# The last two layers of an attention, soft-MoE and feed-forward kernel: the elementwise work of a tile goes over the scalar engine or the vector engine, and GpSimd has no part in it

## The chip, the cores and the metric

The kernel runs on one core of a Trainium2 chip. The metric is the time of one execution in microseconds (us), as the median of several runs. One execution is also taken by the hardware profiler; its rows are what is read below. The engines are TensorE (PE in the rows, PEld for its weight loads), VectorE (DVE), ScalarE (ACT), GpSimd (POOL) and SyncE (SP, which only issues transfers here).

## The reference

Three stages follow one another: causal attention with a memory term, a soft mixture of experts, and a feed-forward block of two layers with a squared relu. The change lies in the last one.

```python
def reference(...):
    x = attention(q, k, v, M_prev, z_prev, beta)      # 4 x 8 heads, 576 tokens, 64 wide
    x = x.transpose(0, 2, 1, 3).reshape(2304, 512)
    # soft mixture: 32 slots over 8 experts of 4
    logits = x @ phi                                  # 2304 x 32
    slot_out = experts(softmax(logits, axis=0).T @ x) # 32 x 512
    x = softmax(logits, axis=1) @ slot_out            # 2304 x 512
    # feed-forward block: w_in 512 x 2048, w_out 2048 x 512, s and b one number each
    h = x @ w_in
    r = np.maximum(h, 0.0)
    g = s * (r * r) + b
    return (g @ w_out).astype(np.float32)
```

`w_in` and `w_out` come as 64-bit floats.

## The kernel before

The kernel has three stages in order of time. The attention stage (0 to about 250 us) goes over 16 pairs of heads in an order that is written out by hand. The experts' weights are streamed through from about 215 to 302 us. The stage of the last two layers, to which the change belongs, fills the rest. In the first and the last of these GpSimd has elementwise work; it can't read the matmul's sums (PSUM) and works from SBUF only.

**The last two layers.** The product of the mixture with `w_in` is folded: `G` (32 slots by 2048, kept with a high and a low part) is `slot_out @ w_in`, made in six pieces by `g_piece`. A *tile* is 128 hidden units (one `k` of 16) for 384 tokens (one group `g` of 6), so there are 96 tiles. `seq` sets their order: first groups 0 and 1 interleaved (`k` = 0 for both, then `k` = 1, ...: 32 tiles), then groups 2 to 5 one after another (16 tiles each).

For a tile, `first` does one matmul (128x384, line L770) into a PSUM buffer `h`, of which there are two, and then the elementwise work: relu, square, times `s`, plus `b`. The result is needed as two rounded parts, `hi` and `lo` = result − `hi`, since the second matmuls run on rounded 32-bit data (fp32r). `second` then does nine matmuls of 512 columns (L799, L800, L801: three blocks of 128 tokens, each `hi` with the high part of `w_out`, `hi` with its low part, `lo` with the high part), which add up over the 16 `k` in PSUM. Behind the last `k` of a group three copies (L200) bring the sums to SBUF and three transfers write them out.

`P` in the rows is the work buffer `r` of a tile, and `R` the ring of `hi` and `lo`, both with NB = 4 places. `second` is called for the tile three behind that of `first` (AHEAD = 3).

Before the change a letter in the table `cp` says how the elementwise work of a tile is split, by `k` and by group (the third word holds for groups 2 to 5):

- "d": relu on ScalarE (L774), then three operations on VectorE (L785, L786, L787).
- "p": relu and square on ScalarE (L774, L776), then affine step, rounding copy and subtraction on GpSimd (L781, L261, L264).
- "q": the same with the rounding copy on ScalarE (L778), and two operations on GpSimd (L779, L264).

There are 58 tiles of the first kind, 31 of the second and 7 of the third.

**The decoding of `w_out`.** Between the first 32 tiles, `decode_out` turns `w_out` from 64-bit to 32-bit floats in eight rounds of two `k` each: one operation on ScalarE (L181), four on VectorE (L183, L185, L187, L189; 128x1024, the first round in halves), and then for each `k` a rounding copy on ScalarE (L758, the high part) and a subtraction on VectorE (L759, the low part). The buffers are `raw` and `PT` for the 64-bit words, `Q0` and `Q1` for the result, and `w` for both parts. The table `dc` says ahead of which tile a round is called, `gp` the same for the pieces of `G`.

**The order.** In this stage a scheduler sets the order of the instructions of each engine when the program is built, from the code's order and from when it expects operands to be ready; on the chip each engine takes its instructions in that fixed order and waits where an operand isn't there. Where a copy is left open (`evac` with no engine named), it also picks ScalarE or VectorE.

Of the kernel before, what the change touches and what calls it, by code (L numbers as in the profile page):

```python
# [12 lines left out]
AF = mybir.ActivationFunctionType  # L13
ALU = mybir.AluOpType
# [31 lines left out]
T = dict(  # L46
    warm=1,
    wt=[3, 4, 4, 4, 3, 3],
    cp=['pppddppppppqpqqq', 'dpdpppdpqdqddddq', 'pddpddddddddddpp'],
    NB=4,  # L50
    sim=0,
    ge='aaaaaa',
    gc='ananaa',
    dc=[-1, 3, -1, 10, 10, 16, 22, 20],
# [17 lines left out]
def strided(ap, *dims):  # L72

    return bass.AP(ap.tensor, ap.offset, [list(ap.ap[0])] + [list(d) for d in dims])
# [3 lines left out]
def tile_attention_moe_ffn(  # L78
# [16 lines left out]
    PE, ACT, DVE, POOL, SP = nc.tensor, nc.scalar, nc.vector, nc.gpsimd, nc.sync  # L95
# [9 lines left out]
    sbt = keep.tile([128, 2], F32, name="sbt")  # L105
# [149 lines left out]
    def load_rest(p):  # L255
        if p < NPAIR:
            qvm_t[p] = QA[p % 3]
            SP.dma_start(out=qvm_t[p], in_=qvm[p])

    def pool_copy(dst, src):  # L260
        POOL.tensor_scalar(out=dst, in0=src, scalar1=1.0, scalar2=0.0, op0=ALU.mult, op1=ALU.add)  # L261

    def pool_sub(dst, a, b):
        POOL.tensor_tensor(out=dst, in0=a, in1=b, op=ALU.subtract)  # L264

    def feature(p, part):
        q = qvm_t[p][:, 0:S]
# [355 lines left out]
    def ps_h():  # L623
        return pH.tile([128, 512], F32, tag="h", name="h")
# [62 lines left out]
    for b in range(B):  # L687
# [14 lines left out]
            out=csk[:, :, 1:4:2, :], in0=strided(cex[:, 0, 0:1], (NSLOT, 5), (0, 2), (1, NSLOT)),  # L702
            in1=strided(chi[:, 0, 0:1], (NSLOT, 5), (0, 2), (1, NSLOT)), op=ALU.subtract)
# [14 lines left out]
    def G(c0, n):  # L718
        return RC[c0 // 1024][:, c0 % 1024:c0 % 1024 + n]
# [48 lines left out]
    def first(n, g, k):  # L768
        hp = ps_h()
        PE.matmul(hp[:, 0:TG], G(k * 128, 128), cT[:, g * TG:(g + 1) * TG], start=True, stop=True)  # L770
        i = n % NB
        r = PC[:, TG * i:TG * (i + 1)]
        hi, lo = ring[2 * i:2 * i + 2]
        ACT.activation(out=r, in_=hp[:, 0:TG], func=AF.Relu)  # L774
        if T["cp"][min(g, 2)][k] in "pq":
            ACT.activation(out=r, in_=r, func=AF.Square)  # L776
            if T["cp"][min(g, 2)][k] == "q":
                ACT.activation(out=hi, in_=r, func=AF.Identity, scale=sbt[:, 0:1], bias=sbt[:, 1:2])  # L778
                POOL.tensor_scalar(out=r, in0=r, scalar1=sbt[:, 0:1], scalar2=sbt[:, 1:2], op0=ALU.mult, op1=ALU.add)  # L779
            else:  # L780
                POOL.tensor_scalar(out=r, in0=r, scalar1=sbt[:, 0:1], scalar2=sbt[:, 1:2], op0=ALU.mult, op1=ALU.add)  # L781
                pool_copy(hi, r)
            pool_sub(lo, r, hi)
        else:
            DVE.scalar_tensor_tensor(out=r, in0=r, scalar=sbt[:, 0:1], in1=r, op0=ALU.mult, op1=ALU.mult)  # L785
            DVE.tensor_scalar(out=hi, in0=r, scalar1=sbt[:, 1:2], scalar2=0.0, op0=ALU.add, op1=ALU.add)  # L786
            DVE.scalar_tensor_tensor(out=lo, in0=r, scalar=sbt[:, 1:2], in1=hi, op0=ALU.add, op1=ALU.subtract)  # L787
        g_t[g, k] = (hi, lo)
# [23 lines left out]
    for i in range(-1, len(seq) + AHEAD):  # L812
        for k2 in range(8):
            if T["dc"][k2] == i:
                decode_out(k2)
        for j in range(6):
            if T["gp"][j] == i:
                g_piece(j)
        if 0 <= i < len(seq):
            first(i, *seq[i])  # L820
        if i >= AHEAD:
            second(*seq[i - AHEAD])
# [63 lines left out]
```

## Time and profile before

| what | value |
|---|---|
| median of 3 runs | 555.32 us (553.84 to 561.74) |
| the profiled execution | 555.2 us, span of its instructions 553.4 us |
| mean granted clock of TensorE | 0.987 of full speed |
| TensorE busy | 520.3 us (94%) |
| VectorE busy | 365.5 us (66%) |
| ScalarE busy | 280.4 us (51%) |
| GpSimd busy | 172.3 us (31%) |

The span runs from the first to the last instruction; the execution's own time lies 1.8 us above it. A share of busy time is a mean over stages that have different limits, and matmuls are pipelined, so that their rows overlap. What counts for the change is the stretch from about 305 us on.

### The profile page before, as it was taken

To read this page: it belongs to the slowest core of one execution; us is meant where nothing else is said; L and a number is where in the kernel's file an instruction comes from. 1 tells how busy PE (TensorE), PEld (TensorE's weight loads), DVE (VectorE), ACT (ScalarE), POOL (GpSimd) and SP (SyncE) were. 2 spreads that over 40 slices of the span, in tenths; PEclk is the share of its full clock that TensorE was granted. 3 is DMA by queue.
4 is the path that set the end of the run, shared out by engine and by line. 5 is a ranking of instruction groups with operands and counts; after the bars stand their busy time and mean duration, and the time that the engine had idled before them with its cause. 6 is when DMAs were issued, how large, how long until landed. Compare 5 with 4: busy or idle time off the path is not lost.

```text
span 553.4 us, 9319 instructions
## 1 busy us (share of the span) xinstructions
PE 520.3 (94%) x3255; PEld 345.3 (62%) x3255; DVE 365.5 (66%) x917; ACT 280.4 (51%) x743; POOL 172.3 (31%) x212
## 2 busy tenths in 40 slices
PE   3999999999999999989999788879999999999997
PEld 1466665666566656653332456558888888888885
DVE  2788887888788878750430999983367465473770
ACT  2877777777777767510221765453542422423322
POOL 0233331332233333300000469996430411404103
PEclk9999999999999999997999999898999999999999
DMA  8799342424242413789995342400020010100101
GB/s 263 249 334 343 126 148 72 150 72 149 69 152 72 149 50 115 245 300 381 368 358 181 126 153 76 152 1 1 1 114 1 10 48 0 59 0 1 57 1 57
DMA packets 26622, 72.01 MB, mean 130 GB/s; under 512 B 3024, under 2 KB 3152, under 8 KB 26576
## 3 DMA queue, kind: packets, MB, share of 16 engines
q1 hardware_dynamic: 26576, 71.42, 37.2%
q8 instruction: 26, 0.43, 0.3%
q14 instruction: 20, 0.16, 0.1%
HBM read 66.69 MB, written 4.72 MB: 129 GB/s over the span
## 4 chain that ended last, share of the span: by engine, by line
PE 84%; POOL 7%; DVE 4%; issue 2%; DMA 1%; ACT 1%; SPq 0%; POOLq 0%; DVEq 0%; ACTq 0%
PE y L799 10%; PE y L801 10%; PE y L800 10%; PE s L290 9%; PE t L335 8%; PE o L394 7%; PE s L364 4%; PE y L662 3%; PE s L294 3%; PE y L646 3%; POOL P L781 3%; PE h L770 3%; POOL R L264 2%; PE t L338 2%; PE t L429 2%
## 5 line engine op out<-in xcount | busy, mean ns | idle before, releaser
L801 PE MATMUL y<-w,R 128*128 128x512 f32 x288 | 114.2, 397 | 6.0 <-POOL R L264 6.0
L799 PE MATMUL y<-w,R 128*128 128x512 f32 x288 | 115.7, 402 | 3.9 <-POOL R L261 3.6
L800 PE MATMUL y<-w,R 128*128 128x512 f32 x288 | 114.1, 396 | 1.4 <-DVE w L759 1.4
L774 ACT ACTIVATE P<-h 128x384 f32<-128x384 f32 x96 | 47.1, 492 | 123.9 <-PE h L770 123.9
L781 POOL TENSOR_SCALAR P<-P,sbt 128x384 f32<-128x384 f32 x31 | 34.7, 1120 | 194.6 <-ACT P L776 194.6
L785 DVE SCALAR_TENSOR_TENSOR P<-P,sbt 128x384 f32<-128x384 f32 x58 | 45.0, 776 | 58.6 <-ACT P L774 58.4
L316 ACT ACTIVATE P<-P,st 128x256 f32<-128x256 f32 (+3 forms) x128 | 71.0, 556 | 5.8 <-DVE st L302 5.8
L801 PEld LDWEIGHTS y<-w,R 128*128 128x128 f32 x288 | 54.6, 190 | 23.3 <-POOL R L264 9.8
L799 PEld LDWEIGHTS y<-w,R 128*128 128x128 f32 x288 | 54.7, 190 | 18.9 <-POOL R L261 6.7
L302 DVE CUSTOM_DVE_ANT_0 P<-s,cs 128x128 f32<-128x128 f32 (+3 forms) x128 | 58.7, 480 | 10.5 <-PE s L290 6.1
L800 PEld LDWEIGHTS y<-w,R 128*128 128x128 f32 x288 | 54.9, 191 | 10.9 <-DVE w L759 1.7
L335 PE MATMUL t<-cs,P 128*128 128x128 f32 x320 | 46.1, 282 | 0.8 <-DVE raw L204 0.6
L290 PE MATMUL s<-R,Q 64*128 64x256 f32 (+3 forms) x176 | 36.8, 499 | 9.5 <-DMA R<-in_qk_dram 8.8
L264 POOL TENSOR_TENSOR R<-P,R 128x384 fp32r<-128x384 f32 x38 | 43.2, 1138 | 3.2
L335 PEld LDWEIGHTS t<-cs,P 128*128 128x128 f32 x320 | 34.2, 141 | 14.4 <-DVE x L417 8.0
L787 DVE SCALAR_TENSOR_TENSOR R<-P,sbt,R 128x384 fp32r<-128x384 f32 x58 | 36.9, 636 | 5.8 <-DVE R L786 0.5
L329 POOL TENSOR_SCALAR P<-P,st 128x576 f32<-128x576 f32 x16 | 16.2, 1014 | 67.1 <-DVE st L325 51.5
L770 PE MATMUL h<-x,R 128*128 128x384 f32 x96 | 34.4, 358 | 0.6 <-ACT P L774 0.6
L202 ACT ACTIVATE raw<-t 128x128 f32<-128x128 f32 (+2 forms) x64 | 25.5, 432 | 15.4 <-PE t L335 15.4
L423 POOL TENSOR_TENSOR x<-x,M 128x512 f32<-128x512 f32 x15 | 19.2, 1280 | 44.4 <-DVE x L417 44.4
L202 ACT ACTIVATE PT<-t 128x128 f32<-128x128 f32 (+2 forms) x64 | 25.2, 433 | 10.4 <-PE t L335 10.4
L786 DVE TENSOR_SCALAR R<-P,sbt 128x384 fp32r<-128x384 f32 x58 | 26.4, 455 | 5.9
(232 smaller groups left out, 868.9 us busy)
## 6 DMA issues: line engine op xcount, KB each, us to landing
w<-in_w_dram SPq DMA_DIRECT2D x18, 512.0 KB, 7.1
raw<-in_w_in_dram SPq DMA_DIRECT2D x8, 1024.0 KB, 5.4
w<-in_w_dram SPq DMA_DIRECT2D x32, 256.0 KB, 5.4
Q<-in_qvm_dram SPq DMA_DIRECT2D x11, 673.0 KB, 5.6
R<-in_qk_dram SPq DMA_DIRECT2D x32, 144.0 KB, 2.8
out_dram<-P SPq DMA_DIRECT2D x18, 256.0 KB, 2.0
raw<-in_w_out_dram SPq DMA_DIRECT2D x4, 1024.0 KB, 4.8
R<-in_qvm_dram SPq DMA_DIRECT2D x5, 673.0 KB, 6.5
```

Source lines behind the costliest of these rows:

```text
L202: ACT.activation(out=dst, in_=src, func=AF.Copy)
L264: POOL.tensor_tensor(out=dst, in0=a, in1=b, op=ALU.subtract)
L290: PE.matmul(ps[:, 512 * h:512 * h + n], q[r, t * 128:(t + 1) * 128], k[r, 0:n], start=True, stop=True)
L302: DVE.tensor_tensor_reduce(out=Pt[h, t], in0=x, in1=cs[:, C_M2 - n:C_M2], scale=-0.125, scalar=BIG, op0=ALU.add, op1=ALU.min, accum_out=st ...
L316: ACT.activation(out=pt, in_=pt, func=AF.Exp, scale=-1.0, bias=st[:, 18 + c:19 + c], accum_out=st[:, c:c + 1])
L335: PE.transpose(tp[:, kb * 128:(kb + 1) * 128], Pt[i, t][:, kb * 128:(kb + 1) * 128], ident)
L770: PE.matmul(hp[:, 0:TG], G(k * 128, 128), cT[:, g * TG:(g + 1) * TG], start=True, stop=True)
L774: ACT.activation(out=r, in_=hp[:, 0:TG], func=AF.Relu)
L781: POOL.tensor_scalar(out=r, in0=r, scalar1=sbt[:, 0:1], scalar2=sbt[:, 1:2], op0=ALU.mult, op1=ALU.add)
L799: PE.matmul(acc[g, i], hi[:, c], who[k], start=(k == 0), stop=False)
L800: PE.matmul(acc[g, i], hi[:, c], wlo[k], start=False, stop=False)
L801: PE.matmul(acc[g, i], lo[:, c], who[k], start=False, stop=(k == NK - 1))
```

## The change

The table `cp` gets other words, and the kinds "p" and "q" are replaced by one kind "a": relu, square, affine step and rounding copy on ScalarE, and one subtraction on VectorE. The kind "d" stays as it is. In the first 32 tiles three of four `k` are "a" in both groups; in the groups 2 to 5 "a" and "d" alternate. That makes 56 "a" and 40 "d" tiles. The two GpSimd helpers go.

```diff
 T = dict(
...
-    cp=['pppddppppppqpqqq', 'dpdpppdpqdqddddq', 'pddpddddddddddpp'],
+    cp=['aaadaaadaaadaaad', 'aaadaaadaaadaaad', 'adadadadadadadad'],
...
-    def pool_copy(dst, src):
-        POOL.tensor_scalar(out=dst, in0=src, scalar1=1.0, scalar2=0.0, op0=ALU.mult, op1=ALU.add)
-
-    def pool_sub(dst, a, b):
-        POOL.tensor_tensor(out=dst, in0=a, in1=b, op=ALU.subtract)
...
         ACT.activation(out=r, in_=hp[:, 0:TG], func=AF.Relu)
-        if T["cp"][min(g, 2)][k] in "pq":
+        if T["cp"][min(g, 2)][k] == "a":
             ACT.activation(out=r, in_=r, func=AF.Square)
-            if T["cp"][min(g, 2)][k] == "q":
-                ACT.activation(out=hi, in_=r, func=AF.Identity, scale=sbt[:, 0:1], bias=sbt[:, 1:2])
-                POOL.tensor_scalar(out=r, in0=r, scalar1=sbt[:, 0:1], scalar2=sbt[:, 1:2], op0=ALU.mult, op1=ALU.add)
-            else:
-                POOL.tensor_scalar(out=r, in0=r, scalar1=sbt[:, 0:1], scalar2=sbt[:, 1:2], op0=ALU.mult, op1=ALU.add)
-                pool_copy(hi, r)
-            pool_sub(lo, r, hi)
+            ACT.activation(out=r, in_=r, func=AF.Identity, scale=sbt[:, 0:1], bias=sbt[:, 1:2])
+            ACT.activation(out=hi, in_=r, func=AF.Copy)
+            DVE.tensor_tensor(out=lo, in0=r, in1=hi, op=ALU.subtract)
         else:
```

The lines behind the removed helpers move up by 6, and those of the "d" kind and of `second` by 10. In the changed file an "a" tile has L768 (relu), L770 (square), L771 (affine step), L772 (rounding copy) and L773 (subtraction); a "d" tile L768 and L775 to L777; the decoding's last two are L752 and L753, and the matmuls are L764 and L789 to L791.

GpSimd's order ends with the attention stage now. Of the 18 copies of finished sums (L200), which the scheduler places, 1 was on VectorE before and 11 are now.

ScalarE, from the relu of tile 4 on, where the decoding's second and third rounds are copied. Before the change (`raw_2872` and `R_3203` at L202 are pieces of `G`, `w` the high parts of `w_out`, P a tile's work buffer):

```order
L774 ACTIVATE P<-h 128x384
L776 ACTIVATE P<-P 128x384
L202 ACTIVATE raw_2872<-h 128x512
L758 ACTIVATE w<-Q_3222 128x512 x2
L758 ACTIVATE w<-Q_3223 128x512 x2
L202 ACTIVATE R_3203<-h 128x512
```

And in the changed program, at the same place:

```order
L768 ACTIVATE P<-h 128x384
L770 ACTIVATE P<-P 128x384
L771 ACTIVATE P<-P,sbt 128x384
L202 ACTIVATE raw_2872<-h 128x512
L772 ACTIVATE R_3202<-P 128x384
L202 ACTIVATE R_3203<-h 128x512
L752 ACTIVATE w<-Q_3222 128x512 x2
L752 ACTIVATE w<-Q_3223 128x512 x2
```

The affine step and the rounding copy of the tile have come in, and the piece of `G` stands ahead of the four copies of weights, where it stood behind them.

VectorE, at the decoding's second and third rounds, whose results those four copies read (L731 and L725 are pieces of `G`). Before:

```order
L183 TENSOR_SCALAR Q_3222<-Q_3222 128x1024
L185 TENSOR_SCALAR Q_3222<-Q_3222 128x1024
L187 SCALAR_TENSOR_TENSOR Q_3222<-PT,Q_3222 128x1024
L731 TENSOR_TENSOR R_3203<-h,R_3203 64x512
L189 SCALAR_TENSOR_TENSOR Q_3222<-PT,Q_3222 128x1024
L759 TENSOR_TENSOR w<-Q_3222,w 128x512 x2
L759 TENSOR_TENSOR w<-Q_3223,w 128x512 x2
```

And in the changed program:

```order
L183 TENSOR_SCALAR Q_3222<-Q_3222 128x1024
L773 TENSOR_TENSOR R_3204<-P,R_3204 128x384
L185 TENSOR_SCALAR Q_3222<-Q_3222 128x1024
L189 SCALAR_TENSOR_TENSOR Q_3223<-raw,Q_3223 128x1024
L187 SCALAR_TENSOR_TENSOR Q_3222<-PT,Q_3222 128x1024
L773 TENSOR_TENSOR R_3204<-P,R_3204 128x384
L189 SCALAR_TENSOR_TENSOR Q_3222<-PT,Q_3222 128x1024
L725 TENSOR_TENSOR R_3203<-h,R_3203 64x512
L773 TENSOR_TENSOR R_3202<-P,R_3202 128x384
L725 TENSOR_TENSOR R_3203<-h,R_3203 64x512
L753 TENSOR_TENSOR w<-Q_3222,w 128x512 x2
L753 TENSOR_TENSOR w<-Q_3223,w 128x512 x2
```

The subtractions of the tiles 2, 3 and 4 (L773) now stand between the operations of the decoding, each behind a ScalarE copy that it waits for.

ScalarE, tiles 9 to 12, around the copies of the decoding's fourth round. In the changed program:

```order
L768 ACTIVATE P<-h 128x384
L772 ACTIVATE R_3203<-P 128x384
L770 ACTIVATE P<-P 128x384
L771 ACTIVATE P<-P,sbt 128x384
L752 ACTIVATE w<-Q_3223 128x512 x2
L772 ACTIVATE R_3204<-P 128x384
L768 ACTIVATE P<-h 128x384
L770 ACTIVATE P<-P 128x384
L768 ACTIVATE P<-h 128x384
L771 ACTIVATE P<-P,sbt 128x384
```

Before, relus and squares alone stood around that pair of copies. Now it stands between the affine step and the rounding copy of tile 10, so that this tile's high part comes behind whatever the pair waits for.

## Rows read from the trace of the kernel before

**Rows 1.** The page: busy time of the engines; the chain that ended last.

```profile
PE 520.3 (94%) x3255; PEld 345.3 (62%) x3255; DVE 365.5 (66%) x917; ACT 280.4 (51%) x743; POOL 172.3 (31%) x212
...
PE 84%; POOL 7%; DVE 4%; issue 2%; DMA 1%; ACT 1%; SPq 0%; POOLq 0%; DVEq 0%; ACTq 0%
```

**Rows 2.** Stretches: length, busy time of each engine (instructions), granted clock, DMA, GB/s.

```profile
300.00:340.00 40.00, 32.75 (x160) 18.87 (x161) 34.92 (x47) 23.75 (x46) 22.06 (x16) 1.00 0.36 116
340.00:380.00 40.00, 33.38 (x125) 24.34 (x124) 32.14 (x30) 20.51 (x37) 38.24 (x33) 0.91 0.18 69
380.00:540.00 160.00, 160.00 (x715) 133.03 (x714) 94.56 (x157) 56.17 (x110) 40.12 (x54) 1.00 0.07 25
```

**Rows 3.** Timeline of TensorE: start, duration, instruction [idle before and its releaser].

```profile
328.18 0.50 PE L800 MATMUL y<-w,R 128*128 128x512 f32 x1 [1.42 <-DVE w L759]
...
335.51 0.34 PE L770 MATMUL h<-x,R 128*128 128x384 f32 x1
...
348.50 0.63 PE L799 MATMUL y<-w,R 128*128 128x512 f32 x1
...
379.29 0.34 PE L770 MATMUL h<-x,R 128*128 128x384 f32 x1
379.46 0.39 PE L799 MATMUL y<-w,R 128*128 128x512 f32 x1
...
540.80 0.34 PE L770 MATMUL h<-x,R 128*128 128x384 f32 x1
```

**Rows 4.** Waits, 335 to 380 us: total us, times, longest.

```profile
PE y L801 <- POOL R L264: 5.1, 7, 1.2
...
PE y L799 <- POOL R L261: 3.1, 5, 0.9
```

**Rows 5.** Timeline of GpSimd: the affine step at two places.

```profile
350.70 1.81 POOL L781 TENSOR_SCALAR P<-P,sbt 128x384 f32<-128x384 f32 x1
...
407.80 0.67 POOL L781 TENSOR_SCALAR P<-P,sbt 128x384 f32<-128x384 f32 x1 [4.17 <-ACT P L776]
```

**Rows 6.** Timeline of VectorE, 306 to 408 us.

```profile
306.63 0.69 DVE L759 TENSOR_TENSOR w<-Q,w 128x512 fp32r<-128x512 f32 x1
...
310.92 1.15 DVE L786 TENSOR_SCALAR R<-P,sbt 128x384 fp32r<-128x384 f32 x1
...
318.92 1.36 DVE L185 TENSOR_SCALAR Q<-Q 128x1024 int32<-128x1024 int32 x1
...
322.65 1.79 DVE L189 SCALAR_TENSOR_TENSOR Q<-PT,Q 128x1024 int32<-128x1024 int32 x1
325.14 3.59 DVE L759 TENSOR_TENSOR w<-Q,w 128x512 fp32r<-128x512 f32 x4 [0.70 <-ACT w L758]
...
329.48 0.62 DVE L785 SCALAR_TENSOR_TENSOR P<-P,sbt 128x384 f32<-128x384 f32 x1
...
330.62 0.41 DVE L786 TENSOR_SCALAR R<-P,sbt 128x384 fp32r<-128x384 f32 x1
...
334.00 1.22 DVE L187 SCALAR_TENSOR_TENSOR Q<-raw,Q 128x1024 int32<-128x1024 int32 x1
...
407.12 0.69 DVE L200 COPY P<-y 128x512 f32<-128x512 f32 x1
```

**Rows 7.** Timeline of ScalarE, 307 to 379 us.

```profile
307.12 0.51 ACT L774 ACTIVATE P<-h 128x384 f32<-128x384 f32 x1
...
337.29 1.15 ACT L758 ACTIVATE w<-Q 128x512 fp32r<-128x512 f32 x2 [0.36 <-DVE Q L189]
...
343.45 1.13 ACT L181 ACTIVATE Q<-raw 128x1024 f32<-128x1024 f32 x1
...
371.98 0.62 ACT L758 ACTIVATE w<-Q 128x512 fp32r<-128x512 f32 x1
...
376.72 0.49 ACT L774 ACTIVATE P<-h 128x384 f32<-128x384 f32 x1 [2.59 <-PE h L770]
377.24 0.52 ACT L776 ACTIVATE P<-P 128x384 f32<-128x384 f32 x1
377.80 0.71 ACT L778 ACTIVATE R<-P,sbt 128x384 fp32r<-128x384 f32 x1
```

## The prediction

> **What bounds the kernel now.** I begin with the busy shares and the chain of work that ended last [rows 1]. The reader is to see that TensorE is busy for 94% of the span and holds 84% of the chain, and that GpSimd is busy for 31% and yet holds 7% of the chain. So GpSimd matters in some stretch and nowhere else. The stretches [rows 2] say which one. From 380 to 540 us TensorE is busy all of the time at a granted clock of 1.00, 160.00 of 160.00 us, whatever the other engines do. From 340 to 380 us it is busy for 33.38 of 40.00 us at a mean granted clock of 0.91, and GpSimd for 38.24. From 300 to 340 us VectorE is the full one (34.92).
>
> Next the timeline of TensorE [rows 3], read by the matmul at L770, of which each tile of the first layer has one. I call the 96 tiles 0 to 95 in the order of `seq`. Counted from the start of the stage, the row at 335.51 us belongs to tile 10, that at 379.29 to tile 23 and that at 540.80 to tile 95. The last 72 tiles take 540.80 − 379.29 = 161.51 us, or 2.243 us each: the price of a tile when nothing is late. The 13 tiles ahead of them would need 13 × 2.243 = 29.16 us at that price and took 379.29 − 335.51 = 43.78 us. So **14.6 us are lost** between 335 and 379 us. The waits of that stretch [rows 4] put 5.1 + 3.1 = 8.2 us of it on GpSimd, in 12 waits. Another part is clock: after such waits matmul rows of 0.63 us stand there in place of 0.39 (the row at 348.50), which is the lower of the two levels, 1.2 for 2.4 GHz. About 18 matmuls at a distance of 0.43 instead of 0.23 us make some 3 us; the restart after each wait makes up the rest. Ahead of 335 us one long wait is left, 1.42 us for VectorE's L759 at 328.18 us: there the decoding of `w_out` is late.
>
> Last, why GpSimd is late. L781 on the same tile took 1.81 us at 350.70 and 0.67 us at 407.80 [rows 5]. The slow one ran beside a full VectorE, the quick one beside none. VectorE pays in the same way: L786 took 1.15 us at 310.92, while GpSimd worked on tile 0, and 0.41 us at 330.62, when GpSimd was idle [rows 6].
>
> **What goes.** All 31 "p" and 7 "q" tiles lose their GpSimd work. GpSimd has nothing left to do behind the attention stage, so no tile can be late for it: the 14.6 us of the stretch from 335 to 379 us go (a), the waits and the clock that fell behind them alike, if what comes in their place isn't late too.
>
> Ahead of that stretch VectorE gets rid of its company. L189 at 322.65 took 1.79 us, where the same operation alone takes 1.22 (L187 at 334.00); four L759 took 3.59 us at 325.14, where one alone takes 0.69; L786 lost 0.74 us [rows 6]. These come to 0.57 + (3.59 − 4 × 0.69) + 0.74 = 2.1 us. Tile 1 no longer takes the vector path (two operations near 0.62 and one of 0.41, together 1.6 us less), but the subtractions of tiles 0 to 3 are new (4 × 0.55 = 2.2 us) and one copy of a weight piece moves there (0.7). Net this is 2.1 + 1.6 − 2.9 = 0.8 us. Operations that I left out ran slow beside GpSimd too: L185 took 1.36 us at 318.92, more than the dearer L187 takes alone, and three more of that kind stand between 315 and 322 us. The wait at 328.18 us so ends 0 to 3 us earlier; I take 2.0 (b), which gives each of these four 0.3 us. The first tile's high part comes later by ScalarE's chain (below) less GpSimd's, some 0.4 us, in front of that wait, which covers it.
>
> **What comes.** An "a" tile puts four operations on ScalarE and one on VectorE. The rows give the first three [rows 7]: relu 0.49, square 0.52, the affine Identity 0.71 us, with starts 0.52 and 0.56 us apart where one needs the other. The copy of 384 columns has no row; the square of the same size is 0.52 and the copy of 512 columns 0.62, and I take 0.52 as the nearer. The subtraction of 384 columns has none either; the one of 512 columns is 0.69, and GpSimd had it so far, so 0.55 in proportion of the columns with something fixed (bounds 0.4 and 0.69). One after the other the four cost 0.52 + 0.56 + 0.75 + 0.57 = **2.40 us**; where other work stands between, an operation hides 0.09 us of the one before it (two copies in 1.15 against 0.62 for one), so at least 0.49 + 0.52 + 0.71 + 0.52 − 4 × 0.09 = 1.88 us. From relu to low part a tile takes some 2.4 + 0.1 + 0.6 = 3.1 us, and TensorE asks for it three tiles later, at 3 × 2.243 = 6.7 us. Alone, such a tile is never late.
>
> In groups 2 to 5 "a" and "d" alternate. ScalarE needs 2.40 + 0.5 = 2.9 us in a pair of tiles and VectorE 0.55 + 2.0, and TensorE takes 4.49 us for it. Eleven of the 18 copies of finished sums stand on VectorE now, in threes of 3 × 0.69 = 2.1 us once in 16 tiles [rows 6]; that fits as well. I cost this stage at nothing; what hides it is TensorE's own 4.49 us.
>
> The first 32 tiles are tighter, since the decoding of `w_out` is between them. ScalarE has from the relu of tile 0 (307.12 us) to the copy of tile 29, the last "a": 24 × 1.88 to 2.40, 6 relus of "d" tiles at 0.4 (0.49 less what the next hides), seven L181 at 1.04, fifteen L758 at 0.53 and five copies of weight pieces at 0.52. These are 65 to 78 us, ending at 372 to 385 us if it never waits. With (a) and (b) TensorE asks for tile 29 at 335.51 − 2.0 + 22 × 2.243 = 383 us (the row at 335.51 stands just ahead of the nine matmuls of tile 7). Pure load so costs 0 to 2 us. The other cost is waiting in the queues: a pair of L758 stands ahead of the copy of a tile and waits for VectorE's L189, which itself stands behind subtractions that wait for ScalarE's copies. The lead of three tiles, 6.7 us, takes up most of such a wait (one round of L187, L189 and a subtraction is 1.22 + 1.22 + 0.55 = 3.0 us). Both together I put at 2.5 us, with ends at 0 and 8 (c).
>
> The Trainium skill speaks against this edit: "ScalarE: Activation LUTs", section "Rules for kernel authors", wants additions and multiplications on VectorE and not on ScalarE. The rows agree that ScalarE is the slower one (0.71 for the affine step against 0.41), but by them it has room here. By that rule alone the dearer path would be paid in full, which is the third case below.
>
> **Sum.** 553.4 − 14.6 (a) − 2.0 (b) + 2.5 (c) = 539.3 us of span. The profiled execution took 555.2 us for a span of 553.4, and the median of three is 555.3, so 1.8 us are added: **541.1 us**. With the ends of (b) and (c) it is 537.6 to 548.6.
>
> **The rivals.** First, that **ScalarE and VectorE lock step**: each of the five decoding rounds still open behind tile 8 costs TensorE a full round of 3.0 us, since the copy behind L758 is always the next that is needed. That is 15 us in place of 2.5, so 553.6 us: no change. Half of it gives 547. For it speaks that both queues run in a fixed order and name each other in it; against it the lead of 6.7 us, and that ScalarE has up to 10 us less load than time.
>
> Second, that **the clock falls anyway**. The granted clock was 0.91 in this stretch with the waits [rows 2], 1.00 without any from 380 us on. If three or four falls like that at 348 us come back with the short waits of (c), at about 1.6 us each, the time is 546 to 548.
>
> Third, on the slower side, **ScalarE becomes the bound** of the last 64 tiles. This decides from the point at which a pair of tiles costs it 4.49 us instead of 2.9, with affine step and copy at 1.4 us each, and each 0.1 us beyond costs 32 × 0.1 = 3.2 us. For 566.4 us, 2% slower, it has to be 541.1 + 32 × 0.79, a pair at 5.28 us. Nothing in the rows comes near that: the dearest ScalarE row of this size is 0.71.
>
> That GpSimd keeps work in this stage can be left out: the order of its instructions ends with the attention stage.
>
> **How the numbers follow.** The forecast has a chance of 0.64, the first rival 0.25, the second 0.08, the slower one 0.03. I count 2% (544.2 to 566.4 us) as what a measurement of this kernel can tell from no change, its three runs lying 1.4% apart. Of the forecast's range some nine tenths of the chance lie below 544.2, hence 0.58 for faster, 0.39 for no change, 0.03 for slower. The range reaches from the low end of the sum, 537, to 551, which takes in the second rival and the first up to four fifths of its price; what is beyond holds less than 2 in 10.
>
> **What would show it.** In the changed profile TensorE should be busy for more than 9 of 10 us from 335 to 380 at a clock of 1.00, with no wait longer than 1 us; the distance of L770 of tiles 23 and 95 (the L764 of the changed file) should stay at 161.5 us; VectorE's L786 should be near 0.42 us and L189 near 1.22 everywhere; and ScalarE's new affine step near 0.71. Wrong would be waits of TensorE for ScalarE's copy or VectorE's subtraction at every decoding round (the first rival), low clock rows with no waits ahead of them (the second), or a distance over 2.25 us for a tile behind tile 32 (the third).

## The result, and the profile after

The changed kernel takes **537.4 us** (median of four runs, 537.04 to 537.89) against 558.5 us of the kernel before on the same chip (four runs, 553.84 to 562.1): a ratio of 0.963 with an interval of 0.954 to 0.972. Predicted were 541.1 us, with a range of 537 to 551. The profiled execution took 537.04 us, with a span of 535.3.

One thing is needed to read these numbers: the executions of most kernels here fall into two groups some 5 to 7 us apart (two and two before the change, all four in the shorter after it), and the three traces that are of the longer one have TensorE's granted clock near the lower level (0.50 to 0.54 in the rows) from 240 to 260 us, before the stage of the change begins. So below I compare the *distance* from the first to the last of the 96 matmuls of the first layer, which leaves that stretch out. Before the change it was 540.8 − 306.6 = 234.2 us, and after it 523.0 − 306.3 = 216.7: **17.5 us** are the change's, less than the 21 between the medians. Each distance is read from one trace; where the lower clock reaches into the first microseconds of the stage, the text says so.

The page of the changed kernel first: busy time of the engines and the chain that ended last.

```profile
PE 513.2 (96%) x3255; PEld 344.6 (64%) x3255; DVE 346.7 (65%) x930; ACT 338.1 (63%) x855; POOL 67.5 (13%) x105
...
PE 94%; DVE 2%; ACT 2%; DMA 1%; issue 1%; SPq 0%; POOL 0%; DVEq 0%; ACTq 0%; POOLq 0%
```

Against [rows 1], TensorE's share of the chain went from 84 to 94% and GpSimd's from 7 to 0. ScalarE is busy for 58 us more, and its share of the chain is 2% where it was 1%. The stretches of the stage (length, busy time of each engine, granted clock, DMA share, GB/s):

```profile
300.00:340.00 40.00, 36.49 (x184) 23.63 (x177) 34.83 (x55) 35.79 (x73) 0.00 (x0) 1.00 0.38 132
340.00:380.00 40.00, 40.00 (x180) 33.26 (x179) 30.48 (x50) 36.58 (x71) 0.00 (x0) 1.00 0.16 53
380.00:520.00 140.00, 140.00 (x625) 116.40 (x624) 73.83 (x136) 84.21 (x160) 0.00 (x0) 1.00 0.08 29
```

The stretch from 340 to 380 us is full now, 40.00 of 40.00 us at a clock of 1.00, where it had 33.38 at 0.91 [rows 2]. VectorE is nearly as busy as before from 300 to 340 us (34.83), but gets more done in it, as its rows below show. The timeline of TensorE at the rows that answer to [rows 3] (start, duration, instruction, idle time before it and its releaser):

```profile
310.31 0.50 PE L789 MATMUL y<-w,R 128*128 128x512 f32 x1 [0.87 <-ACT R L772]
...
332.49 0.39 PE L789 MATMUL y<-w,R 128*128 128x512 f32 x1
...
334.53 0.34 PE L764 MATMUL h<-x,R 128*128 128x384 f32 x1
...
361.45 0.34 PE L764 MATMUL h<-x,R 128*128 128x384 f32 x1
...
522.97 0.34 PE L764 MATMUL h<-x,R 128*128 128x384 f32 x1
```

Counted from the start of the stage, the row at 332.49 begins the nine matmuls of tile 7, 334.53 is tile 11, 361.45 tile 23 and 522.97 tile 95. From tile 11 to tile 95 there are 84 tiles in 188.44 us, 2.243 us each: from here to the end no time is lost. The waits of TensorE from 308 to 535 us say the same (total us, times, longest):

```profile
PE y L789 <- ACT R L772: 0.9, 1, 0.9
PE h L719 <- ACT P L768: 0.6, 1, 0.6
```

Two waits in all, both before 310.4 us, and where [rows 4] had twelve on GpSimd there is none.

### The profile page after: what moved, and what is told of

Its sections match the earlier page's. It is cut to its first block, busy times and chain, and to the rows that moved or that the text cites. A ratio compares the mean times of both kernels' runs of the same rounds, so it can differ in the third digit from the quotient of the medians.

```text
span 535.3 us, 9261 instructions
## 1 busy us (share of the span) xinstructions
PE 513.2 (96%) x3255; PEld 344.6 (64%) x3255; DVE 346.7 (65%) x930; ACT 338.1 (63%) x855; POOL 67.5 (13%) x105
## 4 chain that ended last, share of the span: by engine, by line
PE 94%; DVE 2%; ACT 2%; DMA 1%; issue 1%; SPq 0%; POOL 0%; DVEq 0%; ACTq 0%; POOLq 0%
PE y L789 13%; PE y L790 12%; PE y L791 12%; PE s L284 9%; PE t L329 8%; PE o L388 8%; PE s L358 4%; PE y L656 4%; PE s L288 3%; PE y L640 3%; PE h L764 3%; PE t L332 2%; PE t L423 2%; PE y L661 2%; PE t L400 1%; PE t L436 1%
## 5 line engine op out<-in xcount | busy, mean ns | idle before, releaser
L789 PE MATMUL y<-w,R 128*128 128x512 f32 x288 | 113.6, 396 | 0.9 <-ACT R L772 0.9
L790 PE MATMUL y<-w,R 128*128 128x512 f32 x288 | 113.1, 393 | 0.0
L791 PE MATMUL y<-w,R 128*128 128x512 f32 x288 | 112.3, 390 | 0.0
L768 ACT ACTIVATE P<-h 128x384 f32<-128x384 f32 x96 | 46.6, 486 | 56.0 <-PE h L764 56.0
L773 DVE TENSOR_TENSOR R<-P,R 128x384 fp32r<-128x384 f32 x56 | 31.1, 556 | 68.2 <-ACT R L772 68.2
L789 PEld LDWEIGHTS y<-w,R 128*128 128x128 f32 x288 | 54.0, 188 | 15.1 <-ACT R L772 1.8
L791 PEld LDWEIGHTS y<-w,R 128*128 128x128 f32 x288 | 54.0, 188 | 13.4 <-issue 0.5
L790 PEld LDWEIGHTS y<-w,R 128*128 128x128 f32 x288 | 54.1, 188 | 8.2 <-issue 0.2
L771 ACT ACTIVATE P<-P,sbt 128x384 f32<-128x384 f32 x56 | 39.6, 708 | 1.5
L202 ACT ACTIVATE raw<-t 128x128 f32<-128x128 f32 (+2 forms) x64 | 25.5, 433 | 15.0 <-PE t L329 14.9
L764 PE MATMUL h<-x,R 128*128 128x384 f32 x96 | 33.5, 351 | 0.6 <-ACT P L768 0.6
L202 ACT ACTIVATE PT<-t 128x128 f32<-128x128 f32 (+2 forms) x64 | 25.2, 434 | 10.4 <-PE t L329 10.4
L770 ACT ACTIVATE P<-P 128x384 f32<-128x384 f32 x56 | 29.4, 525 | 1.5
L772 ACT ACTIVATE R<-P 128x384 fp32r<-128x384 f32 x56 | 29.3, 523 | 1.3
L777 DVE SCALAR_TENSOR_TENSOR R<-P,sbt,R 128x384 fp32r<-128x384 f32 x40 | 24.6, 618 | 3.5
L284 PEld LDWEIGHTS s<-R,Q 64*128 64x128 f32 x176 | 14.3, 193 | 18.1 <-DMA Q<-in_qvm_dram 8.3
L310 ACT ACTIVATION_READ_ACCUMULATOR P<-P,st 128x1 f32 x128 | 25.0, 195 | 0.0
```

The source lines that it names most:

```text
L202: ACT.activation(out=dst, in_=src, func=AF.Copy)
L284: PE.matmul(ps[:, 512 * h:512 * h + n], q[r, t * 128:(t + 1) * 128], k[r, 0:n], start=True, stop=True)
L310: ACT.activation(out=pt, in_=pt, func=AF.Exp, scale=-1.0, bias=st[:, 18 + c:19 + c], accum_out=st[:, c:c + 1])
L771: ACT.activation(out=r, in_=r, func=AF.Identity, scale=sbt[:, 0:1], bias=sbt[:, 1:2])
L789: PE.matmul(acc[g, i], hi[:, c], who[k], start=(k == 0), stop=False)
L790: PE.matmul(acc[g, i], hi[:, c], wlo[k], start=False, stop=False)
```

## The experiments

The theory behind the prediction was that GpSimd is late between 335 and 379 us, and that it is late because VectorE and it slow each other. The rivals were that GpSimd simply has too much work there, that the company of GpSimd hurts by VectorE's delay alone, that the last 64 tiles give part of the gain, and that other splits between ScalarE and VectorE do as well or better. Distances are given against the 216.7 us of the changed kernel and the 234.2 of the one before. In medians and ratios, each kernel stands against the runs of the kernel before on the same chip.

### Which tiles give the gain

**The new words for the first 32 tiles alone**, with the old word and the old code for groups 2 to 5:

```diff
-    cp=['pppddppppppqpqqq', 'dpdpppdpqdqddddq', 'pddpddddddddddpp'],
+    cp=['aaadaaadaaadaaad', 'aaadaaadaaadaaad', 'pddpddddddddddpp'],
```

> Only groups 0 and 1 (the first 32 tiles) have the new kinds; groups 2 to 5 keep the old words with GpSimd. Theory (GpSimd was late in the first 32 tiles alone): 537 to 539 us, as the changed kernel, with TensorE at 2.243 us a tile from 335 us on. Rival (the later 64 tiles gave part of the gain): above 545 us.

Measured: 537.5 us (537.25 to 538.19), a ratio of 0.970 (0.968 to 0.971); the distance is 217.4, 0.7 above the full change. The 0.7 are a lower granted clock in the first microseconds of the stage (0.72 from 306 to 312 us): from the second-layer matmuls behind tile 2 to the last tile both kernels take 210.4 us.

**The new word for the last 64 tiles alone:**

```diff
-    cp=['pppddppppppqpqqq', 'dpdpppdpqdqddddq', 'pddpddddddddddpp'],
+    cp=['pppddppppppqpqqq', 'dpdpppdpqdqddddq', 'adadadadadadadad'],
```

> Only groups 2 to 5 have the new kinds; the first 32 tiles keep GpSimd. Theory: as before the change, 552 to 557 us, with the same waits for L264 and L261 between 335 and 379 us. Rival (part of the gain is in the later tiles): below 548 us.

Measured: 554.8 us (ten runs, 552.79 to 560.16), a ratio of 1.000 (0.996 to 1.004), and a distance of 234.1. The waits of TensorE from 310 to 520 us are for GpSimd again, as in [rows 4]:

```profile
PE y L806 <- POOL R L264: 6.0, 8, 1.2
PE y L804 <- POOL R L261: 3.6, 6, 0.9
PE y L805 <- DVE w L759: 1.4, 1, 1.4
```

So the whole gain comes from the first 32 tiles, and the last 64 cost and give nothing that these runs can tell, as the prediction had it.

### Why GpSimd was late

**Less work for GpSimd.** In the kernel before, the 15 "p" tiles among the first 32 become "q", whose rounding copy is on ScalarE:

```diff
-    cp=['pppddppppppqpqqq', 'dpdpppdpqdqddddq', 'pddpddddddddddpp'],
+    cp=['qqqddqqqqqqqqqqq', 'dqdqqqdqqdqddddq', 'pddpddddddddddpp'],
```

> The old kernel, but in the first 32 tiles each p is a q: the rounding copy goes to ScalarE, GpSimd keeps two of three operations. Theory (GpSimd's load is the bound there): 15 operations of about 0.88 us, 13 us of its work, go, so most of the 14.6 us lost there: 541 to 547 us, GpSimd no longer full from 340 to 380 us. Rival (VectorE, slowed by GpSimd in its decoding, is what TensorE waits for): VectorE is still slowed by the same two operations, above 550 us.

Measured: 547.7 us (ten runs, 545.92 to 553.31), a ratio of 0.990 (0.986 to 0.994), distance 226.2: with 15 of its 59 operations in these tiles gone, 8.0 of the 17.5 us are won; the median lies just past the upper edge of what was expected, and "most of the 14.6 us" it isn't. GpSimd is late still, by 6.1 us in fewer and longer waits:

```profile
PE y L806 <- POOL R L264: 6.1, 5, 2.1
PE y L806 <- DVE R L792: 0.7, 1, 0.7
PE y L805 <- DVE w L759: 0.2, 1, 0.2
```

**GpSimd busy with work that nobody waits for.** The changed kernel, and beside it 24 rounds of the three old GpSimd operations on a buffer of their own. They ran from 276.7 to about 353 us:

```diff
+    idle = place("M", SIZE["M"])
+    i0, i1, i2 = (idle[:, TG * j:TG * j + TG] for j in range(3))
+    POOL.memset(i0, 1.0)
+    for _ in range(24):
+        POOL.tensor_scalar(out=i0, in0=i0, scalar1=sbt[:, 0:1], scalar2=sbt[:, 1:2], op0=ALU.mult, op1=ALU.add)
+        POOL.tensor_scalar(out=i1, in0=i0, scalar1=1.0, scalar2=0.0, op0=ALU.mult, op1=ALU.add)
+        POOL.tensor_tensor(out=i2, in0=i0, in1=i1, op=ALU.subtract)
```

> The changed kernel, and beside the first 32 tiles GpSimd runs 24 rounds of the old three operations on a buffer that nobody reads. Nothing waits for GpSimd, so only its company costs. Theory (GpSimd's own chain was what came late; slowing VectorE is a smaller part): VectorE's rows return to 1.0 to 1.8 us, time 538 to 545 us. Rival (the slowed VectorE was the cause): 548 us and above, with TensorE waiting for VectorE's rows.

Measured: 553.4 us (ten runs, 548.16 to 554.51), a ratio of 0.994 (0.990 to 0.998), and a distance of 226.6, which is 9.9 above the changed kernel. Up to 2.1 us of that are a lower granted clock among the first tiles (0.69 and 0.74 from 312 to 324 us); from the second-layer matmuls behind tile 2 on, 7.8 are left. Even the shortest execution lies above the 545 us that I had allowed at most. VectorE's groups from 310 to 355 us, each shape apart (count, busy us, mean ns, idle before):

```profile
L780 DVE TENSOR_TENSOR R<-P,R 128x384 fp32r<-128x384 f32 x8 | 6.1, 757 | 0.8 <-ACT R L779 0.7
...
L187 DVE SCALAR_TENSOR_TENSOR Q<-raw,Q 128x1024 int32<-128x1024 int32 x2 | 3.1, 1572 | 0.0
L189 DVE SCALAR_TENSOR_TENSOR Q<-raw,Q 128x1024 int32<-128x1024 int32 x2 | 3.0, 1517 | 0.0
```

In the changed kernel these groups have means of 553, 1222 and 1219 ns. The waits of TensorE behind it, from 312 to 540 us, are now for VectorE above all, though no tile needs GpSimd:

```profile
PE y L798 <- DVE R L780: 3.5, 5, 1.7
PE h L771 <- DVE R L725: 1.8, 2, 0.9
PE y L796 <- DVE R L783: 1.3, 1, 1.3
```

My theory here had been that this company is the smaller part; at 7.8 to 9.9 us it is about half of the 17.5, and the waits are the rival's. It comes from few encounters: the stage begins at 313.1 us here, and only 10 of the 24 rounds, 30 operations, run beside it, where GpSimd had 59 before the change. Nor is it the order of the instructions, since TensorE, VectorE and ScalarE take theirs in the order of the changed kernel through the whole stage.

**GpSimd with all of its work, and VectorE without the decoding.** The kernel before, with VectorE's four decoding operations left out in rounds 2 to 8:

```diff
-            for part in range(5):
+            for part in (range(5) if k2 == 0 else range(1)):
```

> The kernel before the change, with VectorE's four decoding operations (L183, L185, L187, L189) left out in rounds two to eight, so the output is not the reference's; GpSimd's tile work stays as it was. Theory now (GpSimd and VectorE slow each other; GpSimd alone would be in time): L781 near 0.67 to 1.1 us in most tiles, no long waits for L264, 536 to 541 us. Rival (GpSimd's own load of 31 p tiles is too much whatever VectorE does): waits and time as before, above 550 us.

Measured: 540.6 and 545.7 us (two runs), a ratio of 0.978 (0.967 to 0.990), and a distance of 218.3, 1.6 above the changed kernel, though GpSimd keeps its 22 of the first 32 tiles. GpSimd's groups from 306 to 385 us:

```profile
L264 POOL TENSOR_TENSOR R<-P,R 128x384 fp32r<-128x384 f32 x20 | 22.1, 1103 | 1.7
L781 POOL TENSOR_SCALAR P<-P,sbt 128x384 f32<-128x384 f32 x15 | 13.5, 897 | 94.8 <-ACT P L776 94.8
L261 POOL TENSOR_SCALAR R<-P 128x384 fp32r<-128x384 f32 x15 | 9.3, 618 | 1.3
L779 POOL TENSOR_SCALAR P<-P,sbt 128x384 f32<-128x384 f32 x5 | 3.3, 663 | 6.7 <-ACT R L778 6.7
```

In the kernel before, the same four had means of 1285, 1671, 884 and 1116 ns from 303 to 380 us. Fifteen "p" and seven "q" tiles so cost GpSimd 15 × (0.90 + 0.62 + 1.10) + 7 × (0.66 + 1.10) = 52 us here, and 15 × (1.67 + 0.88 + 1.29) + 7 × (1.12 + 1.29) = 74 us there; TensorE needs 32 × 2.243 = 72 us for the first 32 tiles. GpSimd's own work fits, and the price it has beside a full VectorE doesn't, even if GpSimd never has to wait for its input. The run takes VectorE's own load away too, so it doesn't separate the two halves of the delay; the changed kernel, in which VectorE keeps the decoding and is in time, shows that this load by itself isn't it.

**One operation for GpSimd in each tile.** The changed kernel, with the subtraction of the "a" tiles among the first 32 on GpSimd:

```diff
-            DVE.tensor_tensor(out=lo, in0=r, in1=hi, op=ALU.subtract)
+            (POOL if g < 2 else DVE).tensor_tensor(out=lo, in0=r, in1=hi, op=ALU.subtract)
```

> The changed kernel with the subtraction of the a tiles of the first 32 on GpSimd in place of VectorE: one GpSimd operation a tile where the old p tile had three, and VectorE has 11 us less to do. If company of GpSimd costs by the time that it runs (24 x 1.0 to 1.3 us here against 24 x 2.2 to 4 us on the idle buffer, which cost 11 us): 540 to 544 us. Rival (only a full GpSimd costs): 537 to 538 us.

Measured: 545.2 us (four runs, 544.39 to 552.19), a ratio of 0.985 (0.976 to 0.994), and a distance of 224.0, 7.3 above the changed kernel, although VectorE gave 24 × 0.553 = 13 us of work away; it is just above the expected time. The timeline shows how. GpSimd from 315 to 321 us:

```profile
317.18 1.02 POOL L773 TENSOR_TENSOR R<-P,R 128x384 fp32r<-128x384 f32 x1 [4.38 <-ACT R L772]
319.23 1.53 POOL L773 TENSOR_TENSOR R<-P,R 128x384 fp32r<-128x384 f32 x1 [1.02 <-ACT R L772]
```

And VectorE:

```profile
315.37 0.69 DVE L185 TENSOR_SCALAR Q<-Q 128x1024 int32<-128x1024 int32 x1
...
317.24 1.52 DVE L183 TENSOR_SCALAR Q<-Q 128x1024 f32<-128x1024 f32 x1
318.68 1.21 DVE L189 SCALAR_TENSOR_TENSOR Q<-raw,Q 128x1024 int32<-128x1024 int32 x1
319.81 1.50 DVE L185 TENSOR_SCALAR Q<-Q 128x1024 int32<-128x1024 int32 x1
```

GpSimd's first subtraction starts at 317.18 and takes 1.02 us, to 318.20. VectorE's L183, which starts just behind it, ends at 318.76: 0.56 us after GpSimd, where alone it takes 0.69 (its mean in the changed kernel). L189 starts at 318.68 and takes its usual 1.21 us, to 319.89; now it is GpSimd's second subtraction, started at 319.23, that takes 1.53 in place of 1.02. It ends at 320.76, and VectorE's L185 behind that, at 321.31, after 1.50 us instead of 0.69. So in these three encounters the two engines don't share the loss: who starts first runs at full speed, and the other stands until it is done. The Trainium skill, "SBUF — State Buffer", section "Who interferes with whom", says this of the pair of memory ports that the two have in common: whoever issues first gets it for the whole instruction, and the other fully blocks. The trace agrees, with the 0.5 and 0.8 us above. The 7.3 us needn't all be this: the scheduler has put the instructions of VectorE and ScalarE into another order here, and TensorE waits 2.1 us for GpSimd's subtraction, 1.7 for the copy L772 (0.9 of it at the first tile, as in the changed kernel) and 1.6 for L752.

### Where the work goes instead

**All of the first 32 tiles on VectorE:**

```diff
-    cp=['aaadaaadaaadaaad', 'aaadaaadaaadaaad', 'adadadadadadadad'],
+    cp=['dddddddddddddddd', 'dddddddddddddddd', 'adadadadadadadad'],
```

> The changed kernel with all of the first 32 tiles as d, so neither GpSimd nor ScalarE has the added work. VectorE gets 24 x (1.4 - 0.5) = 22 us more; it is busy for 65 of the 80 us from 300 to 380 now. Theory (taking GpSimd out is not enough, somebody must have room): VectorE is the bound in that stretch, 544 to 550 us. Rival (taking GpSimd out is all that counts): 537 to 539 us.

Measured: 550.6 us (ten runs, 548.36 to 555.56), a ratio of 0.992 (0.988 to 0.997), and a distance of 227.9. Without any GpSimd 6.3 of the 17.5 us are won, which is just past the poor end of what was expected. VectorE is full (39.45 of 40 us):

```profile
340.00:380.00 40.00, 36.53 (x156) 28.01 (x154) 39.45 (x67) 15.92 (x29) 0.00 (x0) 1.00 0.24 79
```

**All of them on ScalarE and the one subtraction:**

```diff
-    cp=['aaadaaadaaadaaad', 'aaadaaadaaadaaad', 'adadadadadadadad'],
+    cp=['aaaaaaaaaaaaaaaa', 'aaaaaaaaaaaaaaaa', 'adadadadadadadad'],
```

> The changed kernel with all of the first 32 tiles as a. ScalarE gets 8 x (1.9 to 2.4 less 0.4) = 12 to 16 us more; it is busy for 72 of the 80 us from 300 to 380 now. Theory (ScalarE has some 7 us left there and no more): TensorE waits for L772, 541 to 547 us. Rival (ScalarE has room, as the prediction's lower load says): 537 to 539 us.

Measured: 539.5 us (four runs, 539.39 to 545.79), a ratio of 0.974 (0.966 to 0.983), distance 219.6. This is better than I had expected: ScalarE is full for 40 us, and the price is only 2.9. Of these 0.8 are a lower granted clock in the first microseconds of the stage (0.72 from 312 to 318 us); behind it TensorE waits twice for ScalarE's L772, 0.6 and 0.7 us. The stretch:

```profile
340.00:380.00 40.00, 39.33 (x174) 31.84 (x173) 32.24 (x46) 39.97 (x82) 0.00 (x0) 1.00 0.24 79
```

**Half and half in the first 32:**

```diff
-    cp=['aaadaaadaaadaaad', 'aaadaaadaaadaaad', 'adadadadadadadad'],
+    cp=['adadadadadadadad', 'adadadadadadadad', 'adadadadadadadad'],
```

> The changed kernel with a and d alternating in the first 32 tiles too: 8 tiles go back from ScalarE to VectorE. VectorE gets 8 x 0.95 = 7.6 us more and is then busy for some 73 of the 80 us from 300 to 380, ScalarE for 57. Theory (VectorE has room as long as GpSimd is silent): 537 to 540 us, and the distance from the first to the last L764 between that of the changed kernel (216.7 us) and that with d alone (227.9). Rival (VectorE is at its limit already): 541 us and above.

Measured: 542.6 us (four runs, 541.99 to 547.2), a ratio of 0.979 (0.971 to 0.987), distance 221.2, 4.5 above the changed kernel. I had expected no more than about 540, so the figure is the rival's. TensorE's timeline from 312 to 380 us has three waits again:

```profile
324.29 0.96 PE L789 MATMUL y<-w,R 128*128 128x512 f32 x3 [1.31 <-ACT w L752]
...
327.04 0.45 PE L764 MATMUL h<-x,R 128*128 128x384 f32 x1 [0.89 <-DVE R L725]
...
344.05 0.44 PE L764 MATMUL h<-x,R 128*128 128x384 f32 x1 [1.30 <-ACT P L768]
```

All three stand in the decoding: a copy and a relu on ScalarE and a piece of `G` on VectorE that come late. Between 340 and 380 us VectorE is busy for 35.5 of 40 us, against 30.5 in the changed kernel, and ScalarE for 29.7 against 36.6, so the fuller engine is VectorE. That its load is the cause isn't shown: two of the three waits are for ScalarE, which isn't full, and the order of both engines is another than in the changed kernel.

**"a" in all 96 tiles:**

```diff
-    cp=['aaadaaadaaadaaad', 'aaadaaadaaadaaad', 'adadadadadadadad'],
+    cp=['aaaaaaaaaaaaaaaa', 'aaaaaaaaaaaaaaaa', 'aaaaaaaaaaaaaaaa'],
```

> The changed kernel with a in all 96 tiles. In the last 64 tiles the four ScalarE operations of a tile follow one another at starts 0.52, 0.56, 0.74 and 0.43 us apart, 2.25 us a tile, where TensorE takes 2.243: the point at which the prediction's third rival begins to decide. Theory (the price of a tile is what the rows say): the distance of the matmuls at L764 stays under 2.27 us and the time lies 0 to 2 us above the kernel with a in the first 32 tiles alone (539.5 us): 539 to 542 us. Rival (a full ScalarE adds waits of its own, as with its copies of sums between the tiles): 2.4 us a tile and 549 us.

Measured: 540.2 us (four runs, 539.45 to 546.27), a ratio of 0.977 (0.966 to 0.987), distance 218.8. From the second-layer matmuls behind tile 2 on it takes 212.5 us, as the kernel with "a" in all of the first 32 tiles alone does. In the last 64 tiles ScalarE is now busy for 96% of the time, and TensorE doesn't wait once:

```profile
420.00:520.00 100.00, 100.00 (x448) 83.15 (x447) 30.72 (x54) 95.67 (x180) 0.00 (x0) 1.00 0.07 24
```

None of these beats the changed kernel (the new words for the first 32 tiles alone equal it), and from 310.4 us on no split could: its TensorE waits for nothing any more.

## Why the prediction was right, and where it was off

**The direction and the range** held, and the mechanism was the one named. The forecast was 3.7 us too long, by two terms of the sum in the main.

**(a), the lost time of 14.6 us between 335 and 379 us**, was right to the tenth: tiles 11 to 23 take 361.45 − 334.53 = 26.92 us for 12 tiles, 2.243 each, with the waits and the low clock gone together. By the second rival the clock would have fallen anyway; it stood at 1.00, with no wait to follow.

**(b), VectorE freed of its company ahead of that**, was given 2.0 us and measured 2.9. From the first matmul of the stage to the nine matmuls of tile 7 it is 332.49 − 306.31 = 26.2 us now; before, they stood behind the row at 335.51 [rows 3], 0.17 later, and it was 335.68 − 306.64 = 29.0. (The rows themselves lie 3.2 apart, but 0.3 of that is the stage's earlier start.) This is just within the bound of 3 that I had set. The operations of the decoding that I priced run alone as said: VectorE's groups of the changed kernel from 303 to 370 us (count, busy us, mean ns, idle before).

```profile
L773 DVE TENSOR_TENSOR R<-P,R 128x384 fp32r<-128x384 f32 x20 | 11.0, 553 | 2.1 <-ACT R L772 2.0
L753 DVE TENSOR_TENSOR w<-Q,w 128x512 fp32r<-128x512 f32 x16 | 10.2, 687 | 1.5 <-ACT w L752 1.5
...
L189 DVE SCALAR_TENSOR_TENSOR Q<-raw,Q 128x1024 int32<-128x1024 int32 x4 | 4.9, 1219 | 0.0
...
L776 DVE TENSOR_SCALAR R<-P,sbt 128x384 fp32r<-128x384 f32 x6 | 2.4, 415 | 0.1
```

They answer to [rows 6]: L189 at 1.22 where it took 1.79, a subtraction of a weight at 0.69 where four took 3.59, L776 at 0.42 where it took 1.15. The subtraction of 384 columns, guessed at 0.55, is 0.553. One reading of mine was wrong without harm: the row at 334.00 that I took for L187 alone has GpSimd's L781 beside it, and there it is GpSimd that stands, for 3.38 us (the row from GpSimd below). The four operations that I had left out had been given 0.3 us each. Three of them in the kernel before, and then GpSimd's row:

```profile
316.38 1.58 DVE L189 SCALAR_TENSOR_TENSOR Q<-raw,Q 128x1024 int32<-128x1024 int32 x1
317.89 1.00 DVE L183 TENSOR_SCALAR Q<-Q 128x1024 f32<-128x1024 f32 x1
...
320.31 1.58 DVE L187 SCALAR_TENSOR_TENSOR Q<-PT,Q 128x1024 int32<-128x1024 int32 x1
```

```profile
332.21 3.38 POOL L781 TENSOR_SCALAR P<-P,sbt 128x384 f32<-128x384 f32 x1 [5.24 <-ACT P L776]
```

With L185 at 318.92 [rows 6] they lost 0.36 + 0.31 + 0.36 + 0.67 = 1.7 us against the 1.22 and 0.69 that they take now, and not 1.2. Yet VectorE's four subtractions of weights end only 1.6 us sooner in the stage, since a fifth subtraction of a tile and one more piece of `G` stand ahead of them: before, at 325.14 + 3.59 − 306.64 = 22.1 us from its start [rows 6], and now at 324.26 + 2.50 − 306.31 = 20.5, by this row of the changed kernel.

```profile
324.26 2.50 DVE L753 TENSOR_TENSOR w<-Q,w 128x512 fp32r<-128x512 f32 x4
```

Something of the 2.9 us came from a place where the prediction hadn't looked, GpSimd's late parts of the very first tile. TensorE in the kernel before:

```profile
310.32 0.50 PE L799 MATMUL y<-w,R 128*128 128x512 f32 x1 [0.55 <-POOL R L261]
...
311.91 0.51 PE L801 MATMUL y<-w,R 128*128 128x512 f32 x1 [0.86 <-POOL R L264]
```

These two waits and the 1.42 us for L759 became the one of 0.87 us for ScalarE's copy. The order of TensorE's matmuls changed there too, so that what each part gave can't be told.

**(c), the new waits in the queues**, was given 2.5 us within 0 to 8 and measured 0: TensorE has no wait from 310.4 us on. This is the step that failed most. The prices of ScalarE's operations were right; its groups over the whole kernel:

```profile
L771 ACT ACTIVATE P<-P,sbt 128x384 f32<-128x384 f32 x56 | 39.6, 708 | 1.5
L770 ACT ACTIVATE P<-P 128x384 f32<-128x384 f32 x56 | 29.4, 525 | 1.5
L772 ACT ACTIVATE R<-P 128x384 fp32r<-128x384 f32 x56 | 29.3, 523 | 1.3
```

I had taken 0.71, 0.52 and 0.52. But the waits that I feared stay inside the lead. At the place that the order showed, the rounding copy of tile 10 stands behind a pair of weight copies; the timeline of ScalarE there:

```profile
333.95 0.56 ACT L770 ACTIVATE P<-P 128x384 f32<-128x384 f32 x1
334.55 0.71 ACT L771 ACTIVATE P<-P,sbt 128x384 f32<-128x384 f32 x1
335.17 1.15 ACT L752 ACTIVATE w<-Q 128x512 fp32r<-128x512 f32 x2
336.21 0.51 ACT L772 ACTIVATE R<-P 128x384 fp32r<-128x384 f32 x1
```

The pair costs this tile 1.04 us and its high part is there at 336.72. TensorE takes it up behind the matmul of tile 13, at 334.53 + 2 × 2.243 + 0.17 = 339.2 us, 2.5 us later. I had named the lead of 6.7 us as what takes up most of such a wait, and then priced the rest all the same; with this split it takes up all of it. That isn't so of every split: with 8 more "a" tiles there are two waits of 0.6 and 0.7 us, and with 8 fewer there are three others of 0.9 to 1.3. The first rival, the lock step of the two engines, is this mechanism at full price, and in the changed kernel it doesn't occur once. (Half of its price would have been 541.1 − 2.5 + 7.5 = 546.1 us, not the 547 that I gave.)

With the measured terms the sum is 553.4 − 14.6 − 2.9 = 535.9 us of span, and 535.3 were measured: the stage began 0.3 us earlier, and what follows the last tile was 0.3 shorter.

**The third rival**, ScalarE as the bound of the last 64 tiles, had its point at 4.49 us for a pair of tiles. "a" in all tiles brings ScalarE to 96% of TensorE's time and costs nothing there, so the point lies where it was put, or beyond; what happens past it wasn't tried.

**Why GpSimd was late** the prediction had in one sentence, and the runs bear it out and sharpen it. Its own load would fit (distance +1.6 with VectorE quiet), VectorE's would fit (the changed kernel), and together they exclude each other, so that each is late on account of the other (+7.8 to 9.9 when no tile needs what GpSimd does, +7.3 with one GpSimd operation in a tile). How the 17.5 us split between tiles that were late from GpSimd and decoding that was late from VectorE stays open: each of these runs changes the number and the places of the encounters, and their costs can't be added.

The Trainium skill's rule against additions and multiplications on ScalarE ("ScalarE: Activation LUTs", section "Rules for kernel authors") would have chosen the tiles that are all "d". The measurement goes the other way, 537.4 against 550.6 us, since it was VectorE that was full. The Trainium skill, "Perfetto Trace Analysis", section "Optimizing Scalar/DVE Operations", has that exception: with VectorE saturated, work may go to ScalarE, while moving it between VectorE and GpSimd might not help.

## What to carry to other kernels

An engine that appears late in the waits may be late because of a neighbour: compare one instruction's duration at a place where the neighbour is busy and at one where it is idle, before counting its load. Here GpSimd beside a full VectorE costs both, even when nothing waits for what it does, so elementwise work that VectorE and GpSimd split can be dearer than the same work on ScalarE, which has the longer instruction and no such neighbour here: its square of a tile takes 0.525 us in the mean beside a busy GpSimd (303 to 380 us before) and without. New waits in a queue count only beyond the lead that the consumer gives, so work the lead out first; whether a queue stays within it depends on its load and order, as the splits above show, and a sum alone doesn't tell.

## What the runs showed of the hardware that was not expected

- GpSimd work that nobody reads (24 rounds of three operations on 128x384) lengthens a stage of 216.7 us by 7.8 to 9.9, with only 30 of the 72 operations beside it. I had expected less.
- The exclusion was all or nothing for an instruction in the encounters read above, either way round: L185 took 0.69 us alone and 1.50 when GpSimd was ahead of it, GpSimd's subtraction 1.02 and 1.53 when L189 was. It needn't be one instruction only: in the kernel before, an affine step of GpSimd that takes 0.67 us alone took 3.38 from 332.21 us on, while VectorE ran four operations at their usual 0.68, 0.61, 0.61 and 1.22.
- ScalarE at 96% busy over 100 us (95.67 of 100.00) delayed TensorE by nothing, while with VectorE at 35.5 of 40 us and ScalarE at 29.7 both were late for it. What differs is that the decoding, the pieces of `G` and the tiles follow each other across both engines there, and that the last 64 tiles have none of it; I take that for the reason, but no run tried it by itself.
